# Attention with a feed-forward layer on one Trainium2 core: two scalars spread by a matmul, another opening order, and eight weight slices prepared in fewer steps

## The chip, the cores and the metric

The kernel runs on one core of a Trainium2 chip. The time is the device time of one execution in microseconds (us), given as the median of several. The core's engines have queues of their own: TensorE multiplies matrices (PE in the profile, with PEld for its weight loads), VectorE (DVE) and ScalarE (ACT) work element by element, GpSimd (POOL) does so too, and SyncE (SP) issues most DMAs. Each engine takes its instructions in the order in which the program lists them.

## The reference

Local attention with a few global keys, and then a feed-forward layer without a gate. Cut to what matters:

```python
B, H, S, D = 4, 8, 768, 64                     # n_global = 8, n_local = 96
scores = q @ k.T / sqrt(D) - slopes * dist     # per head; dist from the diagonal, n_local for global keys
keep = (pos_k < n_global) | ((rel >= 0) & (rel < n_local))
a = softmax(where(keep, scores, -1e9))
x = (a @ v) as (B * S, H * D)                  # 3072 x 512
h = x @ w_in                                   # 512 x 2048
out = where(h > 0, h, exp(min(h, 0)) - 1) @ w_out
```

All data is float64 or float32 on the host; w_in and w_out arrive as float64 and are turned into float32 on the chip. n_global and n_local are two int64 values that the kernel reads at run time.

## The kernel before, in words

The 3072 rows are 12 groups of 256. A group's attention is done in 4 pairs of heads: a load of q and k (tile qk) and of v (tiles v, u), a scaling of q (L449 to L453), 16 score matmuls (s, L474), a fused add-and-minimum against a table of distances (pr, L462, DVE), an exponential with a running sum (L464, ACT), a reciprocal, a normalisation (L449 to L453), transposes on PE (t), their copies (pt) and the product with v (pv). The result is kept as two float32r parts (xh, xl), since a float32 product is made of three float32r ones.

The feed-forward layer's weights are 16 slices each of w_in and w_out, 512 KB of float64 bits a slice (tile bits). `weight` turns a slice into float32 in seven steps: ACT takes the absolute value of the high words read as float32 (L393), DVE or POOL clamps it (L395), DVE shifts it left by 3 and masks it (L396), DVE puts the sign and top bit back (L398) and the upper bits of the low words in (L400), then the high part is copied (w HI, L303 or L305) and the low part subtracted (w LO, L311, POOL).

A planner (`Plan`) sets the order on every engine: each operation has a due time, costs on the engines that may run it, and tiles with a list of slots; the planner simulates and writes down the order that it finds. It starts from numbers for when each engine (FREE) and the DMA stream (BW0) become free. SP's queue is one list: a DMA that waits holds back all that are listed after it. The first three groups are computed while the weights are prepared (the opening); from then on groups alternate between the two matmul layers, and the last eight groups use `seven`, a product with seven instead of eight terms, whose mixed weights (mix) are loaded again for each group.

Ahead of the planned work stands `setup`. It builds the two distance tables far0 and far1 and a small table tabg, which need n_global and n_local. The two scalars come by a DMA that spreads 16 bytes over 128 partitions (n_raw, issued on ACT's queue, L232), are turned to float32 (n_up, n_val, L240 and L242) and applied to the tables (L364 to L372). PE meanwhile runs eight matmuls on a tile of ones (none<-fill, L1113), which compute nothing that is used. Later, where the planner foresees PE idle for more than a bound, further such fills are put in (L1106 and L1113).

At the end a flag is summed from checks of the data; if one fails, a slow path (`dense`) recomputes everything. With this input it is not taken.

Of the kernel before, what the change touches and what calls it, by code (L numbers as in the profile page):

```python
# [8 lines left out]
F32 = mybir.dt.float32  # L9
# [50 lines left out]
class Plan:  # L60
# [5 lines left out]

    BW0 = 2250.0

    FREE = {"PE": 5200.0, "ACT": 3600.0, "DVE": 5300.0, "POOL": 6000.0, "SP": 700.0}

# [165 lines left out]
def scalars(nc, pool, raw):  # L236

    n = raw.shape[1]
    up = pool.tile([P, n], F32, name="n_up")
    nc.vector.scalar_tensor_tensor(up, raw[:, :, 0], 0.0, raw[:, :, 1], ALU.is_lt, ALU.add)  # L240
    val = pool.tile([P, n], F32, name="n_val")
    nc.vector.scalar_tensor_tensor(val, up, float(2 ** 32), raw[:, :, 0], ALU.mult, ALU.add)  # L242
    return [val[:, i:i + 1] for i in range(n)]


class Kernel:
# [67 lines left out]
    def consts(self):  # L314
        self.ident = self.const("ident", [P, P])
        self.far0, self.far1 = self.const("far0", [P, LW]), self.const("far1", [P, LW])

        self.scale = self.const("scale", [P, self.NP])
        if self.ON_PE:
            self.minus1 = self.const("minus1", [P, P], F32R)  # L320
        self.nmax = self.const("nmax", [P, self.B * self.H * self.S // P])
        self.zero = self.const("zero", [P, W], F32R)
        self.sums = {x: self.c.tile([P, 2 * NT, 4], F32, name=x) for x in self.SLOTS["st"]}

    def setup(self):
# [15 lines left out]
        nc.scalar.activation(t, t, AF.Exp)  # L341
        if self.WARM:
            self.fill = m.tile([P, 512], F32R, tag="xh2a", name="fill")
            nc.vector.memset(self.fill.bitcast(F32), 1.0)
            self.none = self.ps.tile([P, 512], F32, tag="h1", name="none")

        for r, at in halves:
# [6 lines left out]
        nc.scalar.copy(far0, far1)  # L354
        nc.vector.tensor_copy(g, j)
        for h in range(0, self.H, 2):
            nc.gpsimd.memset(self.scale.t[:, h // 2:h // 2 + 1], self.q_scale(h))
        nc.gpsimd.tensor_scalar(self.scale.t[HW:], self.scale.t[HW:], 2.0, 1.0, ALU.mult, ALU.mult)
        for r, at in halves:
            nc.gpsimd.memset(far0[r, :at - 32], -BIG)  # L360
            nc.gpsimd.memset(far0[r, at:at + NG], -BIG)
        self.ng, self.nl = scalars(nc, self.c, self.raw)
        ng, nl = self.ng, self.nl
        nc.vector.tensor_scalar(d, d, nl, -BIG, ALU.is_ge, ALU.mult)  # L364
        nc.vector.tensor_scalar(g, g, ng, -BIG, ALU.is_ge, ALU.mult)
        nc.vector.tensor_tensor(far0, far0, d, ALU.add)
        nc.vector.tensor_scalar(g, g, nl, None, ALU.subtract)
        nc.vector.tensor_tensor(far1, far1, d, ALU.add)
        for r, at in halves:
            x = far0[r, at - 32:at - 32 + NG]  # L370
            nc.vector.tensor_tensor(x, x, g[r], ALU.max)
            nc.gpsimd.tensor_copy(far1[r, at:at + NG], g[r])  # L372
        make_identity(nc, self.ident.t)
        nc.gpsimd.memset(self.zero.t.bitcast(F32), 0.0)
        if self.ON_PE:
            nc.scalar.activation(self.minus1.t, self.ident.t, AF.Copy, scale=-1.0)
        for x in self.sums.values():
            nc.gpsimd.memset(x[:, :, 1], 1e-9)


    def weight(self, which, fc, due, after):
# [10 lines left out]

        p.add((("ACT", 575.0, False),), lambda e: nc.scalar.activation(gf(), high().bitcast(F32), AF.Abs), [bits], [g], due - 6000)  # L393
        p.add(dve(DM, True) + (("POOL", 640.0, True),),
              lambda e: self.on(e).tensor_scalar(gf(), gf(), F64_MAX, F64_MIN, ALU.min, ALU.max), [g], [g], due - 5500)  # L395
        p.add(dve(DM, True), lambda e: nc.vector.tensor_scalar(g.t, g.t, 3, 0x3FFFFFFF, ALU.logical_shift_left, ALU.bitwise_and),  # L396
              [g], [g], due - 5000)
        p.add(dve(DM, port=True), lambda e: nc.vector.scalar_tensor_tensor(g.t, high(), -0x40000000, g.t, ALU.bitwise_and, ALU.bitwise_or),  # L398
# [22 lines left out]


    def pair(self, b, gi, hp, xh, xl, due, step, X):
        nc, p = self.nc, self.plan
# [4 lines left out]
        loads = [p.add(sp(), lambda e: nc.sync.dma_start(qk.t, src[:, :W + KS]), writes=[qk], due=due - 9000, nbytes=P * (W + KS) * 4)]  # L429
        loads += [p.add(sp(), lambda e: nc.sync.dma_start(v.t, src[:, W + KS:W + KS + VC]), writes=[v], due=due - 9000, nbytes=P * VC * 4)]  # L430
        if hp % 2 == 0:
            u = self.rest = self.sb("u", "u", [P, VC], slots=X.get("u"))
            loads += [p.add(sp(), lambda e: nc.sync.dma_start(u.t, src[:, W + KS + VC:]), writes=[u], due=due - 9000, nbytes=P * VC * 4)]
        u = self.rest
# [494 lines left out]
    def build(self):  # L929
# [47 lines left out]
        for (n, f0, f1), d in zip(segs, dues):  # L977
            def moe(n=n, f0=f0, f1=f1, d=d):
                b, gi = groups[n]
                if f0 == 0 and f1 < NFC:  # L980
                    parts[n] = [self.sb("part", "part", [P, self.DM]) for _ in range(NT)]
                if n >= self.SE:
                    self.seven(b * self.S + gi * W, *X[n], d, self.STEP, n == len(groups) - 1)
                    return
                self.moe(b * self.S + gi * W, *X[n], f0, f1, d, self.STEP, parts.get(n), n < self.NE, n == len(groups) - 1)
            todo.append((d[f0], moe))
        self.kept, self.mixed = {}, {}
        for j in range(NFC // 2):
# [4 lines left out]
        for _, f in sorted(todo, key=lambda x: x[0]):  # L993
# [28 lines left out]
    SLOTS = {"qk": ["rqv0", "qk0"], "v": ["va1", "va2"], "u": ["rk0", "va0"], "s": ["s0", "s1"], "t": ["t0"], "pv": ["v0", "t0"], "h": ["h0", "h1"], "o0": ["o0"], "o1": ["o1"],  # L1022
             "pr": ["pr0", "pr1", "pr2", "pr3"], "tr": ["pt0", "pt1"], "pt4": ["ph0", "ph1"], "dd": [f"dd{i}" for i in range(4)], "st": [f"st{i}" for i in range(6)], "pt": ["pt0", "pt1"],
             "x": ["x0"], **{x + c: [f"{x}{n}{c}" for n in range(3)] for x in ("xh", "xl") for c in "ab"}, "e": ["e0", "e1"], "gh": ["gh0", "gh1", "gh2"],
             "gl": ["gl0", "gl1", "gl2"], "io": ["io0", "io1", "io2", "io3"], "part": [f"pa{i}" for i in range(6)], "mix": [f"pa{i}" for i in range(6)],  "hl": ["xh0a", "xh0b"], "tf": ["tf0", "tf1", "xl0a", "xl0b"],
             "g": ["io2", "io3"], "sum7": ["ph2", "x0"], "rh": ["gh0", "gh1"], "rl": ["gl0", "gl1"], "sh": ["xh2a", "xl2a"], "sl": ["xh2b", "xl2b"], "o2": ["v0"], "o3": ["t0"], "o4": ["s0"], "o5": ["s1"]}
# [11 lines left out]
    def run(self):  # L1038
# [3 lines left out]
        with self.tc.manual_schedule():  # L1042
# [4 lines left out]
            self.setup()  # L1047
            free = self.warm(self.COLD * 240.0, 0.0)
            cold = min(op.n for op in order if op.eng == "PE" and op.allocs and op.allocs[0].cls == "h")
# [68 lines left out]
    def flag(self):  # L1118
# [10 lines left out]
        nc.vector.tensor_scalar(f[:, 5:6], f[:, 5:6], 1.0, None, ALU.is_lt)  # L1129
        nc.vector.tensor_reduce(f[:, 6:7], f[:, 0:6], axis=AX.X, op=ALU.max)  # L1130
        one = c.tile([P, 1], F32, name="one")
# [3 lines left out]
    def flag_sum(self, flags):  # L1135
        nc, c = self.nc, self.c
        f, one = flags
        s = self.ps.tile([P, 1], F32, tag="s0", name="flagsum")
        nc.tensor.matmul(s[0:1, :], f[:, 6:7], one, start=True, stop=True)
# [113 lines left out]
    def restored(self):  # L1253
        M = self.DM // 2
        for j, x in self.kept.items():
            self.nc.sync.dma_start(self.ws[1][2 * j].t[:, :, M:].bitcast(F32), x.t)

    def dense(self, b):
        for t0 in range(0, self.S // P, NT):
            self.dx = [self.p.tile([P, self.NCC, W], F32R, tag=f"dx{i}", name=self.n("dx")) for i in range(2)]  # L1260
            for i in range(NT):
                self.dense_tile(b, t0 + i, i)
            self.dense_moe(b, t0)

# [77 lines left out]
```

## Time and profile before

| | us |
|---|---|
| median of 3 runs (lowest to highest) | 645.14 (643.47 to 645.53) |
| the profiled execution, time | 644.23 |
| the profiled execution, span | 642.4 |
| PE busy | 631.0 (98%) |
| DVE busy | 492.7 (77%) |
| ACT busy | 411.0 (64%) |
| POOL busy | 199.1 (31%) |

The span is the stretch from the profile's first instruction to its last; the execution's time is 1.8 us more. PE's busy time counts the fills too, and a matmul counts as busy until its modelled end.

### The profile page before, as it was taken

The numbers are of one execution on the slowest core, as the hardware profiler recorded it, in microseconds if no ns is written. First come the engines' busy times: TensorE is split into PE (matmuls) and PEld (weight loads), VectorE is DVE, ScalarE is ACT, GpSimd is POOL, SyncE is SP. The second block draws the span as 40 slices with busy tenths as digits, with TensorE's granted clock in tenths as the row PEclk, the third lists the DMA queues.
The fourth block names the chain that finished last, engine by engine and source line by source line (L and its number), as shares of the span: only waits on it lengthen the run. The fifth ranks groups of instructions, "written<-read, shape, count | busy, mean of one in ns | idle before, by whom it ended". The sixth has DMA issues, their size and how long they took to land.

```text
span 642.4 us, 19164 instructions
## 1 busy us (share of the span) xinstructions
PE 631.0 (98%) x7054; PEld 584.4 (91%) x7054; DVE 492.7 (77%) x1648; ACT 411.0 (64%) x1201; POOL 199.1 (31%) x500
## 2 busy tenths in 40 slices
PE   8999999999999999999999999999999999999996
PEld 5878888898888889999999999999999999999996
DVE  6999888899878975777777777777686777776654
ACT  6999776666644665666666566576566566654553
POOL 3557465465467672121121121112022022020000
PEclk9999999999999999999999999999999999999998
DMA  8979934231365899788888888888888788875542
GB/s 309 376 283 408 342 84 125 70 108 62 87 220 211 260 300 295 250 269 246 270 252 282 258 251 264 277 259 253 273 253 243 254 283 260 277 233 165 181 149 86
DMA packets 131171, 149.82 MB, mean 233 GB/s; under 512 B 63616, under 2 KB 82816, under 8 KB 131072
## 3 DMA queue, kind: packets, MB, share of 16 engines
q1 hardware_dynamic: 130784, 148.41, 71.7%
q8 instruction: 57, 0.93, 0.6%
q14 instruction: 42, 0.34, 0.2%
q10 hardware_dynamic: 288, 0.13, 0.1%
HBM read 117.57 MB, written 30.93 MB: 231 GB/s over the span
## 4 chain that ended last, share of the span: by engine, by line
PE 89%; DVE 4%; ACT 3%; DMA 2%; issue 1%; POOL 0%; DVEq 0%; POOLq 0%; ACTq 0%
PE h L712 28%; PE o L768 24%; PE o L880 13%; PE h L854 12%; PE s L610 5%; PE s L474 4%; PE pv L507 2%; DMA qk<-in_qkv_dram 1%; ACT pr L464 1%; PE t L527 1%; DMA n_raw<-in_n_dram 1%; DVE pr L462 1%; DMA mixed<-mix 1%; PE t L529 0%; DVE g L395 0%
## 5 line engine op out<-in xcount | busy, mean ns | idle before, releaser
L712 PE MATMUL h<-xh,w 128*128 128x256 f32 x1024 | 142.2, 280 | 0.8 <-DVE gg L722 0.8
L712 PEld LDWEIGHTS h<-xh,w 128*128 128x128 f32 x1024 | 129.8, 188 | 3.0 <-issue 1.2
L722 DVE SCALAR_TENSOR_TENSOR gg<-e,h 128x256 f32<-128x256 f32 x128 | 53.4, 417 | 76.0 <-ACT e L721 74.9
L580 POOL TENSOR_SCALAR pr<-pr,st 128x168 f32<-128x168 f32 x144 | 62.6, 435 | 152.1 <-DVE st L482 139.3
L464 ACT ACTIVATE pr<-pr,nmax 128x168 f32<-128x168 f32 x192 | 81.8, 427 | 16.9 <-DVE nmax L462 16.3
L720 ACT ACTIVATE e<-h 128x256 f32<-128x256 f32 x128 | 48.7, 381 | 58.4 <-PE h L712 58.4
L854 PEld LDWEIGHTS h<-xh,w 128*128 128x128 f32 x512 | 76.9, 188 | 9.9 <-DVE h L862 0.2
L880 PE MATMUL o<-w,gh 128*128 128x512 f32 x256 | 81.6, 400 | 0.4 <-DVE ob L912 0.4
L712 PE MATMUL h<-xl,w 128*128 128x256 f32 x512 | 81.8, 281 | 0.0
L854 PE MATMUL h<-xh,w 128*128 128x256 f32 x512 | 81.5, 282 | 0.0
L712 PEld LDWEIGHTS h<-xl,w 128*128 128x128 f32 x512 | 69.4, 188 | 2.0 <-issue 1.7
L462 DVE CUSTOM_DVE_ANT_0 pr<-s,far 128x168 f32<-128x168 f32 x192 | 53.3, 325 | 11.8 <-ACT xh L303 11.1
L311 POOL TENSOR_TENSOR w<-g,w 128x256 fp32r<-128x256 f32 x64 | 50.8, 816 | 35.7 <-ACT w L303 29.8
L303 ACT CAST sh<-sum 128x512 fp32r<-128x512 f32 x64 | 39.8, 621 | 30.9 <-DVE sum L736 30.9
L585 DVE STREAM_TRANSPOSE tr<-pr 128x192 f32<-128x192 f32 x144 | 50.0, 364 | 11.2 <-POOL pr L580 10.7
L721 ACT ACTIVATE e<-e 128x256 f32<-128x256 f32 x128 | 53.4, 417 | 3.6
L768 PE MATMUL o<-mix,sh 128*128 128x256 f32 x256 | 51.1, 281 | 0.0
L880 PEld LDWEIGHTS o<-w,gh 128*128 128x128 f32 x256 | 43.0, 188 | 7.9 <-ACT e L860 1.0
L451 POOL TENSOR_SCALAR qk<-qk,scale 128x256 f32<-128x256 f32 x14 | 8.0, 570 | 135.6 <-DMA qk<-in_qkv_dram 68.1
L311 DVE TENSOR_TENSOR sl<-sum,sh 128x512 fp32r<-128x512 f32 x64 | 44.2, 691 | 5.7 <-ACT sh L303 5.7
L768 PE MATMUL o<-w,sh 128*128 128x256 f32 x256 | 48.1, 280 | 0.0
L303 ACT CAST rh<-gg 128x384 fp32r<-128x384 f32 x64 | 32.8, 513 | 20.1 <-DVE gg L722 19.5
(142 smaller groups left out, 1418.9 us busy)
## 6 DMA issues: line engine op xcount, KB each, us to landing
mix<-mixed SPq DMA_DIRECT2D x192, 256.0 KB, 4.6
qk<-in_qkv_dram SPq DMA_DIRECT2D x48, 312.0 KB, 4.1
v<-in_qkv_dram SPq DMA_DIRECT2D x36, 384.0 KB, 5.0
dd<-tr SPq DMA_DIRECT2D x36, 384.0 KB, 4.6
pt<-dd SPq DMA_DIRECT2D x72, 192.0 KB, 3.8
bits<-in_w_in_dram SPq DMA_DIRECT2D x16, 512.0 KB, 8.5
bits<-in_w_out_dram SPq DMA_DIRECT2D x16, 512.0 KB, 9.7
mixed<-mix SPq DMA_DIRECT2D x32, 256.0 KB, 3.2
```

The source lines that it names most:

```text
L303: self.nc.scalar.copy(out, x)
L311: self.on(e).tensor_tensor(out, x, y, ALU.subtract)
L462: first = p.add((("DVE", 85 + 1.042 * LW, False),), lambda e: nc.vector.tensor_tensor_reduce(x(), s.t[:, i, :LW], tab, -(2.0 ** -(h + 1)), ...
L464: p.add(act(LW, extra=200), lambda e: nc.scalar.activation(x(), x(), AF.Exp, bias=nm, scale=-1.0, accum_out=st.t[:, n, 0:1]), [pr], [pr, s ...
L580: nc.gpsimd.tensor_scalar(pr.t[:, :LW], pr.t[:, :LW], st.t[:, n, 3:4], 1.0, ALU.mult, ALU.mult)
L585: nc.vector.transpose(tr.t[:, :, i, j], pr.t.rearrange("p (b r) -> p b r", r=32))
L712: nc.tensor.matmul(h.t, w1.t[:, s, cc * P:(cc + 1) * P], self.chunk(x, cc), start=n == 0 and s == HI and cc == 0, stop=n == 1 and cc == se ...
L721: p.add(act(W), lambda e: nc.scalar.activation(ex.t, ex.t, AF.Exp, scale=-1.0), [ex], [ex], d - 8000)
L722: p.add(dve(W), lambda e: nc.vector.scalar_tensor_tensor(gs(), ex.t, -1.0, h.t, ALU.add, ALU.max), [h, ex], [g], d - 8000)
L768: nc.tensor.matmul(acc[bank].t[:, half], a, b.t[:, LO if t == 1 else HI, x], start=j == 0 and t == 0 and n in first, stop=j == self.NFC // ...
L854: nc.tensor.matmul(h.t, w1.t[:, s, cc * P:(cc + 1) * P], self.chunk(x, cc), start=n == 0 and cc == 0, stop=n == 2 and cc == self.NCC - 1)
L880: nc.tensor.matmul(o.t[:, :at.stop - at.start], g.t[:, i * P:(i + 1) * P], w2.t[:, s, at], start=fc == f0 and n == 0 and s == HI, stop=fc ...
```

## The change

**Scalars.** n_raw is loaded into one partition. n_up and a new n_one are made there; a matmul with the tile of ones (fill) spreads the two values over 128 partitions (n_all in PSUM), and DVE copies them out (n_val). The eight fills at the start become three ahead of this matmul and two behind it.

**Opening order.** Work on tabg moves from DVE to POOL; the identity and the zero tile are made ahead of the scalars' arrival; far1 is finished behind far0. The planner's FREE and BW0 are smaller, and the first group's v and u loads have due times 9000 later, so that a second qk load stands ahead of them.

**Weights.** For the slices 0 to 3 of w_in and of w_out (BARE = 4, eight slices) the absolute value (L393) and the clamp (L395) are left out, and the shift (L396) reads the high words straight out of the raw bits.

**Check.** From planner time 251000 on, every 12000, half a slice of those raw words is loaded again (tile seen, 16 loads of 256 KB), and ACT runs two activations over its 256 high words a partition with a running sum into a column of `wide`. `flag` takes 32 columns into its result with 4 more DVE instructions. The slow path gets a function `rewritten` that prepares the eight slices in full; it is not run here.

```diff
-    BW0 = 2250.0
-    FREE = {"PE": 5200.0, "ACT": 3600.0, "DVE": 5300.0, "POOL": 6000.0, "SP": 700.0}
+    BW0 = 1200.0
+    FREE = {"PE": 4100.0, "ACT": 3000.0, "DVE": 4400.0, "POOL": 4600.0, "SP": 700.0}
...
-    raw = pool.tile([P, n, 2], I32, name="n_raw")
-    nc.scalar.dma_start(raw, src.bitcast(I32).rearrange("(o n w) -> o n w", o=1, w=2).broadcast_to([P, n, 2]))
+    raw = pool.tile([1, n, 2], I32, name="n_raw")
+    nc.scalar.dma_start(raw, src.bitcast(I32).rearrange("(o n w) -> o n w", o=1, w=2))
...
+    one = pool.tile([1, n], F32, name="n_one")
+    nc.vector.scalar_tensor_tensor(one, up, float(2 ** 32), raw[:, :, 0], ALU.mult, ALU.add)
+    all_ = psum.tile([P, n], F32, tag="h0", name="n_all")
+    nc.tensor.matmul(all_, ones[0:1, :P], one, start=True, stop=True)
     val = pool.tile([P, n], F32, name="n_val")
-    nc.vector.scalar_tensor_tensor(val, up, float(2 ** 32), raw[:, :, 0], ALU.mult, ALU.add)
+    nc.vector.tensor_copy(val, all_)
...
+        self.warm(self.COLD[0] * 240.0, 0.0)
+        self.ng, self.nl = scalars(nc, self.c, self.raw, self.fill.bitcast(F32), self.ps)
+        ng, nl = self.ng, self.nl
+        nc.gpsimd.tensor_scalar(g, g, ng, -BIG, ALU.is_ge, ALU.mult)
+        nc.gpsimd.tensor_scalar(g, g, nl, 0.0, ALU.subtract, ALU.add)
+        nc.vector.tensor_scalar(d, d, nl, -BIG, ALU.is_ge, ALU.mult)
+        nc.vector.tensor_tensor(far0, far0, d, ALU.add)
...
+        bare = fc < self.BARE
+        if not bare:
+            p.add((("ACT", 575.0, False),), lambda e: nc.scalar.activation(gf(), high().bitcast(F32), AF.Abs), [bits], [g], due - 6000)
+            p.add(dve(DM, True) + (("POOL", 640.0, True),),
+                  lambda e: self.on(e).tensor_scalar(gf(), gf(), F64_MAX, F64_MIN, ALU.min, ALU.max), [g], [g], due - 5500)
+        p.add(dve(DM, True), lambda e: nc.vector.tensor_scalar(
+            g.t, high() if bare else g.t, 3, 0x3FFFFFFF, ALU.logical_shift_left, ALU.bitwise_and), [bits if bare else g], [g], due - 5000)
...
+    def watch(self, k, due):
...
+        src = (self.w_in, self.w_out)[which][fc].bitcast(I32)[:, half * DM:(half + 1) * DM]
+        x = self.sb("seen", "seen", [P, DM], I32)
+        p.add(sp(), lambda e: nc.sync.dma_start(x.t, src), writes=[x], due=due - 4000, nbytes=P * DM * 4, early=due - 4000)
...
+        p.add(act(DM // 2, extra=200), lambda e: nc.scalar.activation(t(), t(), AF.Abs, accum_out=w[:, k:k + 1]), [x], [x], due, slack=8000.0)
+        p.add(act(DM // 2, extra=200), lambda e: nc.scalar.activation(t(), t(), AF.Exp, scale=-512.0, accum_out=w[:, n + k:n + k + 1]), [x], [x], due)
...
-    GATE, COLD = 900.0, 8
+    GATE, COLD = 900.0, (3, 2)
...
+    BARE, WATCH = 4, (255000.0, 12000.0)
```

On DVE's queue the opening stood thus before, from the third table step (far is a distance table, tabg the small table) to the first fused step of attention (L462):

```order
L353 SCALAR_TENSOR_TENSOR far_71<-d,after 128x168
L355 CAST tabg<-tabj 128x8
L240 SCALAR_TENSOR_TENSOR n_up<-n_raw 128x2
L242 SCALAR_TENSOR_TENSOR n_val<-n_up,n_raw 128x2
L364 TENSOR_SCALAR d<-d,n_val 128x168
L365 TENSOR_SCALAR tabg<-tabg,n_val 128x8
L366 TENSOR_TENSOR far_70<-far_70,d 128x168
L367 TENSOR_SCALAR tabg<-tabg,n_val 128x8
L368 TENSOR_TENSOR far_71<-far_71,d 128x168
L371 TENSOR_TENSOR far_70<-far_70,tabg 64x8 x2
L462 ISA pr_184,nmax<-s_168,far_70 128x168
```

and thus in the changed program, on the same queue:

```order
L356 SCALAR_TENSOR_TENSOR far_71<-d,after 128x168
L240 SCALAR_TENSOR_TENSOR n_up<-n_raw 1x2
L242 SCALAR_TENSOR_TENSOR n_one<-n_up,n_raw 1x2
L246 COPY n_val<-n_all 128x2
L374 TENSOR_SCALAR d<-d,n_val 128x168
L375 TENSOR_TENSOR far_70<-far_70,d 128x168
L378 TENSOR_TENSOR far_70<-far_70,tabg 64x8 x2
L379 TENSOR_TENSOR far_71<-far_71,d 128x168
L473 TENSOR_SCALAR qk_151<-qk_151,scale 128x256
L482 ISA pr_183,nmax<-s_166,far_70 128x168
```

The three steps on tabg have left DVE; a copy that waits for PE has come in, and so has the scaling of the second pair's q (L473), which before stood on POOL (L451) behind the memsets.

On ACT's queue of the changed program the first of the sixteen checks stands thus in the late stage (e is the activation of the feed-forward layer, rh and sh its rounded parts, seen the raw words):

```order
L307 CAST rh_4599<-gg_4517 128x384
L307 CAST sh_4605<-sum_915_4585 128x512
L469 ACTIVATE qk_4529<-qk_4529,scale 128x256
L740 ACTIVATE e_4629<-h_4590 128x256
L440 ACTIVATE seen_4390,wide<-seen_4390 128x256
L741 ACTIVATE e_4629<-e_4629 128x256
L441 ACTIVATE seen_4390,wide<-seen_4390 128x256
L740 ACTIVATE e_4658<-h_4615 128x256
L741 ACTIVATE e_4658<-e_4658 128x256
```

The two rows of seen are new; they stand between the two steps of e, and between one e and the next.

## Rows read from the trace of the kernel before

**Rows 1.** The page: an engine's busy time over the whole span.

```profile
PE 631.0 (98%) x7054; PEld 584.4 (91%) x7054; DVE 492.7 (77%) x1648; ACT 411.0 (64%) x1201; POOL 199.1 (31%) x500
```

**Rows 2.** Waits of PE after the opening: releaser, us in total, times, longest.

```profile
PE h L712 <- DVE gg L722: 0.8, 1, 0.8
PE o L880 <- DVE ob L912: 0.4, 1, 0.4
```

**Rows 3.** Busy time in three stretches; then clock, DMA share, GB/s.

```profile
core 0: us, PE busy (x) PEld busy (x) DVE busy (x) ACT busy (x) POOL busy (x), PEclk, DMA share, GB/s
6.00:46.00 40.00, 37.88 (x503) 29.19 (x504) 36.68 (x159) 36.24 (x127) 20.31 (x44) 1.00 0.92 344
46.00:60.00 14.00, 13.90 (x198) 11.28 (x198) 13.24 (x51) 13.38 (x49) 11.36 (x17) 1.00 1.03 410
250.00:450.00 200.00, 200.00 (x2493) 193.51 (x2492) 147.04 (x541) 128.27 (x374) 32.04 (x132) 1.00 0.84 261
```

**Rows 4.** The same view for the fills alone (tile none): PE, PEld.

```profile
6.00:46.00 40.00, 6.87 (x28) 4.11 (x28) 1.00 0.92 344
```

**Rows 5.** Timeline of the first 9 us: start, duration, engine, what, idle before.

```profile
0.83 0.40 ACTq L232 DMA_DIRECT2D n_raw<-in_n_dram  x1
...
1.55 3.78 PE L1113 MATMUL none<-fill 128*128 128x512 f32 x8 [1.55 <-DVE fill L344]
...
2.46 0.33 DVE L353 SCALAR_TENSOR_TENSOR far<-d,after 128x168 f32<-128x168 f32 x1
...
4.92 0.16 DVE L240 SCALAR_TENSOR_TENSOR n_up<-n_raw 128x2 f32<-128x2 int32 x1 [2.05 <-DMA n_raw<-in_n_dram]
...
5.32 0.31 DVE L364 TENSOR_SCALAR d<-d,n_val 128x168 f32<-128x168 f32 x1
5.32 0.51 ACT L449 ACTIVATE qk<-qk,scale 128x256 f32<-128x256 f32 x1 [2.16 <-DMA qk<-in_qkv_dram]
...
5.88 1.21 PE L474 MATMUL s<-qk 64*64 64x168 f32 x16 [0.56 <-ACT qk L449]
...
6.89 0.33 DVE L462 CUSTOM_DVE_ANT_0 pr<-s,far 128x168 f32<-128x168 f32 x1
...
8.02 0.48 POOL L451 TENSOR_SCALAR qk<-qk,scale 128x256 f32<-128x256 f32 x1
...
8.56 0.80 PE L474 MATMUL s<-qk 64*64 64x168 f32 x16 [0.34 <-POOL qk L451]
```

**Rows 6.** DMA queues in the first 5 us: packets, MB, share.

```profile
q1 hardware_dynamic: 224, 0.48, 33.6%
q10 hardware_dynamic: 144, 0.00, 1.3%
```

**Rows 7.** DMA issues of the page: count, KB, us from issue to landing.

```profile
mixed<-mix SPq DMA_DIRECT2D x32, 256.0 KB, 3.2
```

**Rows 8.** Groups by line, 10 to 46 us: busy us, mean ns | idle before.

```profile
L393 ACT ACTIVATE g<-bits 128x512 f32<-128x512 f32 x8 | 5.2, 671 | 0.0
L398 DVE SCALAR_TENSOR_TENSOR g<-bits,g 128x512 int32<-128x512 int32 x6 | 4.2, 706 | 0.1
...
L395 POOL TENSOR_SCALAR g<-g 128x512 f32<-128x512 f32 x5 | 3.0, 614 | 1.8 <-ACT g L393 1.7
L396 DVE TENSOR_SCALAR g<-g 128x512 int32<-128x512 int32 x6 | 2.4, 416 | 0.0
L395 DVE TENSOR_SCALAR g<-g 128x512 f32<-128x512 f32 x3 | 2.0, 680 | 0.0
```

**Rows 9.** Groups by line on ACT, 255 to 440 us.

```profile
L721 ACT ACTIVATE e<-e 128x256 f32<-128x256 f32 x60 | 25.0, 417 | 1.6
...
L464 ACT ACTIVATION_READ_ACCUMULATOR pr<-pr,nmax 128x1 f32 x64 | 12.0, 188 | 0.0
```

**Rows 10.** Timeline of the late stage: sl is made, and read next.

```profile
273.69 0.69 DVE L311 TENSOR_TENSOR sl<-sum,sh 128x512 fp32r<-128x512 f32 x1
...
276.66 0.19 PEld L768 LDWEIGHTS o<-mix,sl 128*128 128x128 f32 x1
```

More of the change, by code (lines that the diff above doesn't have):

```diff
@@ L341, in setup @@
         nc.scalar.activation(t, t, AF.Exp)
[L342 to L345, printed above, removed]
+        self.fill = m.tile([P, 512], F32R, tag="xh2a", name="fill")
+        nc.vector.memset(self.fill.bitcast(F32), 1.0)
+        self.none = self.ps.tile([P, 512], F32, tag="h1", name="none")
         for r, at in halves:
@@ L361, in setup @@
             nc.gpsimd.memset(far0[r, at:at + NG], -BIG)
[L362 to L372, printed above, removed]
         make_identity(nc, self.ident.t)
@@ L376, in setup @@
             nc.scalar.activation(self.minus1.t, self.ident.t, AF.Copy, scale=-1.0)
+        self.warm(self.COLD[0] * 240.0, 0.0)
[5 more added lines that the diff above has]
+        nc.vector.tensor_tensor(far0, far0, d, ALU.add)
+        for r, at in halves:
+            x = far0[r, at - 32:at - 32 + NG]
+            nc.vector.tensor_tensor(x, x, g[r], ALU.max)
+        nc.vector.tensor_tensor(far1, far1, d, ALU.add)
         for x in self.sums.values():
             nc.gpsimd.memset(x[:, :, 1], 1e-9)
+        for r, at in halves:
+            nc.gpsimd.tensor_copy(far1[r, at:at + NG], g[r])
     def weight(self, which, fc, due, after):
@@ L429, in pair @@
         loads = [p.add(sp(), lambda e: nc.sync.dma_start(qk.t, src[:, :W + KS]), writes=[qk], due=due - 9000, nbytes=P * (W + KS) * 4)]
-        loads += [p.add(sp(), lambda e: nc.sync.dma_start(v.t, src[:, W + KS:W + KS + VC]), writes=[v], due=due - 9000, nbytes=P * VC * 4)]
+        loads += [p.add(sp(), lambda e: nc.sync.dma_start(v.t, src[:, W + KS:W + KS + VC]), writes=[v], due=due - 9000 + X.get("later", 0), nbytes=P * VC * 4)]
         if hp % 2 == 0:
             u = self.rest = self.sb("u", "u", [P, VC], slots=X.get("u"))
-            loads += [p.add(sp(), lambda e: nc.sync.dma_start(u.t, src[:, W + KS + VC:]), writes=[u], due=due - 9000, nbytes=P * VC * 4)]
+            loads += [p.add(sp(), lambda e: nc.sync.dma_start(u.t, src[:, W + KS + VC:]), writes=[u], due=due - 9000 + X.get("later", 0), nbytes=P * VC * 4)]
         u = self.rest
@@ L986, in build @@
             todo.append((d[f0], moe))
+        for k in range(4 * self.BARE):
+            d = self.WATCH[0] + k * self.WATCH[1]
+            todo.append((d - 4000.0, lambda k=k, d=d: self.watch(k, d)))
         self.kept, self.mixed = {}, {}
@@ L1047, in run @@
             self.setup()
-            free = self.warm(self.COLD * 240.0, 0.0)
+            free = self.warm(self.COLD[1] * 240.0, 0.0)
             cold = min(op.n for op in order if op.eng == "PE" and op.allocs and op.allocs[0].cls == "h")
@@ L1138, in flag_sum @@
         s = self.ps.tile([P, 1], F32, tag="s0", name="flagsum")
-        nc.tensor.matmul(s[0:1, :], f[:, 6:7], one, start=True, stop=True)
+        nc.tensor.matmul(s[0:1, :], f[:, 7:8], one, start=True, stop=True)
         fi = c.tile([1, 1], I32, name="flagint")
@@ L1256, in restored, with rewritten @@
             self.nc.sync.dma_start(self.ws[1][2 * j].t[:, :, M:].bitcast(F32), x.t)
+    def rewritten(self):
+        nc, p, DM = self.nc, self.p, self.DM
+        for fc in range(self.BARE):
+            for which in range(2):
+                bits = p.tile([P, 2 * DM], I32, tag="bits", name=self.n("bits"))
+                g = p.tile([P, DM], I32, tag="bg", name=self.n("bg"))
+                w = self.ws[which][fc].t
+                gf = g.bitcast(F32)
+                words = bits.rearrange("p (n w) -> p n w", w=2)
+                nc.sync.dma_start(bits, (self.w_in, self.w_out)[which][fc].bitcast(I32))
+                nc.scalar.activation(gf, words[:, :, 1].bitcast(F32), AF.Abs)
+                nc.vector.tensor_scalar(gf, gf, F64_MAX, F64_MIN, ALU.min, ALU.max)
+                nc.vector.tensor_scalar(g, g, 3, 0x3FFFFFFF, ALU.logical_shift_left, ALU.bitwise_and)
+                nc.vector.scalar_tensor_tensor(g, words[:, :, 1], -0x40000000, g, ALU.bitwise_and, ALU.bitwise_or)
+                nc.vector.scalar_tensor_tensor(g, words[:, :, 0], 29, g, ALU.logical_shift_right, ALU.bitwise_or)
+                nc.scalar.copy(w[:, HI], gf)
+                nc.vector.tensor_tensor(w[:, LO], gf, w[:, HI], ALU.subtract)
     def dense(self, b):
@@ L1275, in tile_kernel @@
                 f.restored()
+                f.rewritten()
                 with tc.For_i(0, f.B, 1) as b:
```

27 lines of the change are left out of this document (16 added, 11 removed).

## The prediction

> **What bounds the kernel now.** I read the page first: PE is busy for 631.0 us of a span of 642.4 [rows 1]. That alone doesn't say that PE is the limit, since its fills count as work, so the list of PE's waits comes next. After 70 us PE waits for named releasers for 1.2 us in all, in two waits [rows 2]. From there on a change can hardly win anything on DVE, ACT or POOL, and it can lose only if it makes PE wait.
>
> The opening is another matter. The table by stretches for 6 to 46 us shows PE "busy" for 37.88 of 40 us [rows 3], but the same view for the fills alone has 6.87 us of it [rows 4]. So 40 - 37.88 + 6.87 = 9.0 us of PE's time in this stretch do no work that is used. In the same 40 us DVE is busy for 36.68 (92%) and ACT for 36.24 (91%), POOL for 20.31 [rows 3]: two engines that hand each other softmax steps and weight steps are nearly full. From 46 to 60 us PE is at 13.90 of 14 [rows 3] without fills. PE's later work is a fixed queue, so what is won in the opening, by starting sooner or by giving DVE and ACT less to do, moves everything behind it by as much, up to the 9.0 us plus what the start gives.
>
> The start itself is read in the timeline. DVE has its tables prepared at 2.46 + 0.33 = 2.79 and then waits until 4.92 for n_raw; ACT waits 2.16 us for the first qk load, until 5.32; the first fused step of attention on DVE is at 6.89, and the second pair's scores are only at 8.56, behind a scaling that POOL does at 8.02 [rows 5].
>
> **Part 1, the scalars and the opening order.** n_raw was issued at 0.83 and released DVE at 4.92, 4.1 us later [rows 5]. In the first 5 us the queue that carries it moved 144 packets with almost no bytes, against 224 packets of the data queue [rows 6]: spreading 16 bytes over 128 partitions costs 144 of the first 368 packets. With one partition nearly all of these go away. How soon n_raw then lands no row shows. It cannot help before 2.79, when DVE comes free; a transfer of 256 KB takes 3.2 us from issue to landing [rows 7], so 0.83 + 3.2 = 4.0 is a late bound. I take the middle, 3.4.
>
> The DMA: Bandwidth & Descriptors page of the Trainium skill (Anatomy of one DMA) puts the fixed part of a DMA at about 2.0 us, as measured for those that GpSimd issues. By it n_raw would land at about 2.8, at the early bound, and this part would be worth 0.6 us more.
>
> From there: n_up and n_one take 0.40, as n_up and n_val did between 4.92 and 5.32 [rows 5]. Then the new trip through PE, which no row shows: at least 0.3 us (two handovers and a tiny matmul), at most the 1.21 us of the first sixteen score matmuls [rows 5]; a two-column matmul is nearer the low end, 0.5. The fills ahead of it are three of eight that took 3.78 [rows 5], about 1.4 us from 1.55, and are over by then. The copy n_val is about 0.17. From the step on d to the fused step it took 6.89 - 5.32 = 1.57 before [rows 5]; two steps on tabg that leave DVE take about 0.3 of that, and the scaling of the second pair's q, now on DVE ahead of the fused step, adds about 0.35. The sum is 3.4 + 0.40 + 0.5 + 0.17 + 1.27 + 0.35 = 6.1, so 0.8 us sooner, with ends at 5.3 and 7.4 (1.6 us sooner to 0.5 later). The first qk must be there too. It was at 5.32, and with over a third of the packets gone it comes no later; it doesn't decide. What gains more is the second pair: its scaling is done at about 5.8 in place of 8.50, if its load, now second in SP's queue and not fourth, has landed, and its scores follow the first sixteen at about 6.5 to 7, not at 8.56. Between the 0.8 of the first step and the 1.5 to 2 of the second I take **-1.5 us** for the start, bounds -2.1 and +0.5.
>
> **Part 2, the eight weight slices.** All eight are prepared between 10 and 46 us, since the absolute value stands there eight times [rows 8]. What goes: on ACT 8 x 0.671 = 5.4 us; the clamp three times on DVE, 3 x 0.680 = 2.0, and five times on POOL, 5 x 0.614 = 3.1 [rows 8]. What comes: the shift now reads every second word. It took 0.416 on packed words; the step that reads the same high words (L398) takes 0.706 [rows 8]. Between 0 and 0.29 more for each of eight, I take the row that reads the same data: +2.3 us on DVE. So ACT and DVE together lose 5.4 + 2.0 - 2.3 = 5.1 us of work, and POOL 3.1. The planner may give normalisations, scalings and copies to either ACT or DVE, so the relief can be shared: 5.1 / 2 = 2.6 for two engines, (5.1 + 3.1) / 3 = 2.7 if POOL takes its part. The bounds are 0 (DVE alone decides, as it gets +2.3 - 2.0) and 5.4 (ACT alone decides). I take **-2.7 us**; with the start it is well below the 9.0 us that PE can give.
>
> **Part 3, the check in the late stage.** 16 loads of 256 KB and 32 activations. One activation over 256 elements is 0.417 us and its sum's read 0.188 [rows 9], 0.6 together, so 32 x 0.6 = 19 us on ACT within some 190 us, where ACT is busy for 128 of 200 [rows 3]. The loads add 4.2 MB where 261 GB/s x 200 us = 52 MB are moved at a share of 0.84 [rows 3], which becomes about 0.91. What hides them is PE's distance to its inputs. Where four softmax steps already stand among the steps of e, sl is finished at 273.69 + 0.69 = 274.38 and read at 276.66 [rows 10], 2.3 us to spare; a check puts in at most 1.2 us. Queued behind a check that waits for its load is the next e, and for that PE waits; the load is listed on SP about two rounds of mix loads ahead of the round in which it is read. I take **+0.2 us**. Without that cover it would be 16 x 1.2 = 19 us, the upper bound.
>
> The 4 more DVE instructions of the flag stand where DVE is busy for 147 of 200 us [rows 3] and PE doesn't wait: nothing, or under 1 us if that slack were gone. The slow path isn't run.
>
> **The sum.** -1.5 - 2.7 + 0.2 = -4.0 us. The profiled execution took 644.23, so its like would take 640.2. The median of the runs is 0.9 above that execution, 645.14; from it I get **641.1**, and I give 641.0. A difference below 0.3%, 1.9 us, can't be told from none here, so faster means below 643.2.
>
> **The rivals.**
>
> *The loads set the pace.* From 46 to 60 us the DMA share is 1.03, over 6 to 46 it is 0.92 at 344 GB/s [rows 3]. If q, k, v and bits come no sooner, ACT and DVE wait for data with the time they gained, and only what the start moves is kept: -1.3, 643.8, no difference. Against it: the bytes of the opening are the same, and their stream starts with fewer packets. It decides if POOL's and DVE's waits for qk or bits grow by over 2 us.
>
> *The check makes PE wait* (the case on the other side). Two activations are put between two steps of e. If each check held PE up by 0.6 us, one activation, that is 16 x 0.6 = 9.6; with -4.2 for the rest it is +5.4, 650.5. It decides from 4.2 / 16 = 0.26 us a check on. Against it: the 2.3 us to spare, and only 1.2 us of waits after the opening [rows 2, 10].
>
> *PE's clock stays low for longer.* The eight fills end 3.78 us after they began, about 0.43 us apart, which is 512 columns at 1.2 GHz, and the first sixteen score matmuls take 1.21 us against 0.80 for the second [rows 5]: the clock rises to its other level, 2.4 GHz, about then. The changed start has five fills with a wait among them. If the rise came later, each of about five groups of PE work up to 11 us would cost 0.4 us more, 2 us in all: 643.1. The page TensorE: Matmul & The Clock Gate of the Trainium skill (Part 1: The HAM clock gate) says that the array's clock is halved unless it has been busy of late, so that fewer fills speak against the change; the first rows agree that a start from rest is slow.
>
> *More comes of it.* If ACT alone decided, part 2 would be worth 5.4 and the start 2.1: -7.3, 637.8.
>
> **How the numbers follow.** Forecast 0.64, loads 0.14, check 0.08, clock 0.06, more 0.08. The likeliest case alone reaches from 638.8 to 643.0 (2 us for the split of the relief and the start). For 8 in 10 I add the case of the loads and half of the larger gain: 638.0 to 644.5. Faster: the forecast, "more" and half of the clock's and a little of the loads' case, 0.77; the same 0.15; slower 0.08.
>
> **What would show it.** Start: n_raw's wait on DVE ends before 4.0, the first fused step stands at about 6, the second pair's scores before 7.5. Relief: L393 and L395 gone from 10 to 46 us but for later slices, the shift of the eight at 0.6 to 0.7 us, fills plus idle PE from 6 to 46 us at 5 to 6 us in place of 9.0. Check: PE's waits after 70 us still near 1 us. It would be wrong if fills and idle time stay at 9 us (the loads), or if PE waits for gg or sl after each check.

## The result and the profile after

The changed kernel takes 648.4 us (median of 9 executions, 644.81 to 650.4) against 645.14 us before (9 executions on the same chip). The ratio is 1.0056 (95% interval 1.0036 to 1.0076): 3.6 us slower by the ratio, 3.3 by the medians. The forecast was 641.0 (638.0 to 644.5). The profiled execution is the fastest of the nine, 644.81 with a span of 642.9, so its rows show less of the loss than the median has.

The page's busy line (compare [rows 1]) and PE's waits from 70 to 640 us (compare [rows 2]; columns as there):

```profile
PE 629.1 (98%) x7034; PEld 582.5 (91%) x7034; DVE 489.7 (76%) x1639; ACT 417.5 (65%) x1258; POOL 198.5 (31%) x505
```

```profile
PE s L630 <- DMA pt<-dd: 1.5, 3, 0.7
PE o L900 <- ACT e L880: 1.2, 2, 0.7
PE s L630 <- DVE tr L605: 0.3, 1, 0.3
```

PE's waits rise from 1.2 to 3.0 us, and none stands behind gg or sl, where the rival of the check was looked for. They stand at products with v, whose input pt comes back from DRAM (tr is stored as dd and loaded again as pt), and at e in the stage of the mixing.

The table by stretches (columns of [rows 3]), and then the fills alone (compare [rows 4]):

```profile
6.00:46.00 40.00, 37.86 (x501) 28.52 (x498) 36.61 (x156) 35.09 (x129) 19.86 (x38) 1.00 0.95 352
46.00:60.00 14.00, 13.55 (x189) 11.49 (x188) 12.65 (x46) 12.57 (x44) 10.47 (x16) 1.00 1.03 408
186.00:250.00 64.00, 61.86 (x606) 54.11 (x605) 50.36 (x147) 36.48 (x115) 41.58 (x76) 1.00 0.75 239
250.00:450.00 200.00, 198.96 (x2475) 192.19 (x2475) 145.36 (x536) 136.25 (x429) 33.05 (x136) 1.00 0.90 286
```

```profile
6.00:46.00 40.00, 4.68 (x13) 2.10 (x13) 1.00 0.95 352
```

From 6 to 46 us, 40 - 37.86 + 4.68 = 6.8 us of PE do nothing used, where 9.0 did. But from 250 to 450 us PE is idle for 1.04 us, where it had no gap. The stretch from 186 to 250 us, which the prediction did not look at, has 61.86; the same row of the kernel before is

```profile
186.00:250.00 64.00, 63.63 (x621) 56.02 (x620) 51.71 (x150) 35.35 (x112) 41.29 (x80) 1.00 0.82 265
```

so PE is idle there for 1.8 us more. A last part lies behind PE: from the start of its last matmul to the end of the span 6.80 us pass, where 6.05 passed before. The traces have 6.0 to 6.3 us there in the kernel before, e2, e6, e7 and e12, and 6.8 to 7.2 in the others; what sets it stays open. The timeline of the start (compare [rows 5]):

```profile
0.84 0.53 ACTq L232 DMA_DIRECT2D n_raw<-in_n_dram  x1
...
2.73 0.14 DVE L240 SCALAR_TENSOR_TENSOR n_up<-n_raw 1x2 f32<-1x2 int32 x1
...
3.12 0.58 PE L244 MATMUL n_all<-n_one,fill 1*128 1x2 f32 x2
...
3.75 0.16 DVE L246 COPY n_val<-n_all 128x2 f32<-128x2 f32 x1 [0.69 <-PE n_all L244]
3.84 0.51 ACT L469 ACTIVATE qk<-qk,scale 128x256 f32<-128x256 f32 x1 [0.66 <-DMA qk<-in_qkv_dram]
3.94 0.43 DVE L374 TENSOR_SCALAR d<-d,n_val 128x168 f32<-128x168 f32 x1
...
5.52 0.33 DVE L378 TENSOR_TENSOR far<-far,tabg 64x8 f32<-64x8 f32 x2 [0.67 <-POOL tabg L373]
...
6.40 0.33 DVE L482 CUSTOM_DVE_ANT_0 pr<-s,far 128x168 f32<-128x168 f32 x1
...
6.84 1.21 PE L494 MATMUL s<-qk 64*64 64x168 f32 x16
```

DVE no longer waits for n_raw, the first fused step is 0.49 us sooner, the second pair's scores 1.72 us sooner. In the first 5 us n_raw's queue carries 2 packets (144 in [rows 6]), and the first qk releases ACT at 3.84, 1.5 us sooner. The shift of the bare slices, in the groups by line from 10 to 46 us, costs what it did on packed words (0.416 in [rows 8]):

```profile
q10 hardware_dynamic: 2, 0.00, 0.0%
```

```profile
L403 DVE TENSOR_SCALAR g<-bits 128x512 int32<-128x512 int32 x7 | 2.8, 418 | 0.1
```

**Where the lead goes.** PE's work is compared by number: the start of the n-th h<-xh,w matmul (1536 in each trace) minus its start in the trace of before, in us, negative when ahead. The columns say when that matmul starts in the trace of before. Each row is one execution: the changed kernel's and e3's are the fastest of their runs, e1's and e9's near the slowest. Runs e1 to e16 follow below.

| profiled execution | 73 | 181 | 242 | 279 | 318 | 471 | 631 |
|---|---|---|---|---|---|---|---|
| changed | -3.3 | -3.3 | -0.7 | -0.8 | -0.8 | 0.2 | -0.2 |
| changed again (e5) | -2.9 | -2.9 | -0.5 | 0.0 | 1.1 | 3.6 | 3.7 |
| no check (e1) | -3.8 | -3.7 | -1.7 | 0.7 | 1.1 | 2.5 | 2.3 |
| mixing earlier (e3) | -3.0 | -3.0 | -3.2 | -3.2 | -1.4 | -2.0 | -1.8 |
| no check, mixing earlier (e11) | -3.2 | -3.2 | -3.6 | -3.6 | -3.4 | -3.4 | -3.9 |
| mixing earlier, small check (e13) | -1.9 | -1.9 | -2.1 | -2.1 | -1.2 | -2.6 | -3.1 |
| mixing earlier, full loads, small activations (e14) | -1.8 | -1.8 | -2.1 | -2.1 | -0.3 | -0.7 | -0.6 |
| weights only (e4) | 1.8 | 1.7 | 1.8 | 1.8 | 3.6 | 2.2 | 1.5 |
| opening only (e6) | 1.4 | 1.7 | 1.4 | 1.3 | 2.0 | 1.2 | 0.7 |
| PE held (e7) | -2.9 | 0.8 | 2.7 | 3.3 | 3.7 | 6.2 | 6.1 |
| small check (e9) | -2.1 | -2.1 | 0.8 | 1.8 | 2.7 | 2.8 | 2.5 |
| full loads, small activations (e10) | -2.0 | -2.0 | 1.6 | 2.9 | 3.4 | 4.1 | 3.8 |

The opening gives 3.3 us (2.9 in e5, the same kernel again) and PE holds them to 181 us. The changed kernel loses them in two places: the mixing (186 to 245 us) and the stage after it (280 to 440 us).

### The profile page after: what moved, and what is told of

It is laid out like the page before. It is cut to its first block, busy times and chain, and to the rows that moved or that the text cites. A ratio compares the mean times of both kernels' runs of the same rounds, so it can differ in the third digit from the quotient of the medians.

```text
span 642.9 us, 19209 instructions
## 1 busy us (share of the span) xinstructions
PE 629.1 (98%) x7034; PEld 582.5 (91%) x7034; DVE 489.7 (76%) x1639; ACT 417.5 (65%) x1258; POOL 198.5 (31%) x505
## 4 chain that ended last, share of the span: by engine, by line
PE 84%; DMA 4%; DVE 4%; POOL 3%; ACT 2%; issue 2%; SPq 0%; POOLq 0%; DVEq 0%; ACTq 0%
PE h L732 27%; PE o L788 24%; PE o L900 11%; PE h L874 10%; PE s L630 4%; PE s L494 4%; PE pv L527 2%; DMA dd<-tr 2%; DMA pt<-dd 1%; POOL pr L600 1%; DVE mix L315 1%; PE t L547 1%; ACT pr L484 1%; PE none L1137 1%; DMA qk<-in_qkv_dram 1%
## 5 line engine op out<-in xcount | busy, mean ns | idle before, releaser
L315 POOL TENSOR_TENSOR w<-g,w 128x256 fp32r<-128x256 f32 x64 | 48.8, 786 | 42.1 <-ACT w L307 29.0
L471 POOL TENSOR_SCALAR qk<-qk,scale 128x256 f32<-128x256 f32 x14 | 6.7, 478 | 150.4 <-DMA qk<-in_qkv_dram 75.8
```

Source lines behind the costliest of these rows:

```text
L315: self.on(e).tensor_tensor(out, x, y, ALU.subtract)
```

## The experiments

Each run's ratio is to the kernel before on the same chip (medians there 644.11 for e1 to e4, 644.42 for e5 to e8, 645.59 for e9 to e12, 644.31 for e13 to e16). The ratios weigh all executions and are up to 0.0013 off the quotient of the two medians. e13 has 5 executions, e5, e7 and e12 have 6, e10 has 8, the others 11 or 12.

| run | us | ratio (95%) |
|---|---|---|
| e1 no check | 646.51 | 1.0024 (1.0003 to 1.0044) |
| e2 before, with the check | 645.58 | 1.0023 (1.0007 to 1.0040) |
| e3 mixing earlier | 646.34 | 1.0028 (1.0008 to 1.0048) |
| e4 weights only | 644.60 | 1.0006 (0.9989 to 1.0022) |
| e5 changed, again | 648.78 | 1.0080 (1.0052 to 1.0108) |
| e6 opening only | 643.31 | 0.9986 (0.9970 to 1.0003) |
| e7 PE held | 650.58 | 1.0099 (1.0077 to 1.0121) |
| e8 check from 90 us, mixing earlier | 646.61 | 1.0037 (1.0023 to 1.0052) |
| e9 small check | 644.84 | 0.9997 (0.9974 to 1.0020) |
| e10 full loads, small activations | 650.12 | 1.0083 (1.0055 to 1.0111) |
| e11 no check, mixing earlier | 641.94 | 0.9950 (0.9932 to 0.9968) |
| e12 opening only, mixing earlier | 652.01 | 1.0098 (1.0066 to 1.0129) |
| e13 = e3, small check | 640.47 | 0.9941 (0.9927 to 0.9955) |
| e14 = e3, full loads, small activations | 644.42 | 1.0004 (0.9989 to 1.0018) |
| e15 check by 165 us, mixing earlier | 644.67 | 1.0014 (0.9996 to 1.0032) |
| e16 check by 165 us | 643.89 | 0.9990 (0.9970 to 1.0010) |

**The parts alone.** e1 takes the loop over `watch` out of the changed kernel and sets `wide` to zero (the check of those words is left out). e2 is the kernel before with `watch` and the longer flag. e4 is the kernel before with `bare` in `weight` (no check of those words). e6 is the changed kernel with

```diff
-        bare = fc < self.BARE
+        bare = False
```

and no check, which full preparation does not need.

> The changed kernel without the sixteen late loads of raw words and their 32 activations (the columns of the flag that they fill are set to zero instead, so nothing is checked). Theory C (the check costs: its 4.2 MB and 19 us of ACT work make PE wait in the last eight groups): the time falls by 3 to 4 us against the changed kernel, to 644 to 645.5, and the runs lie as close together as those of the kernel before. Theory M (the lead of 3.3 us that the changed kernel has from 70 to 186 us is lost between 186 and 245 us, where the mixed weights are made at fixed planned times and their stores stand in SP's queue between the transfers dd and pt): the lead is still lost by 245 us, and the time stays within 1 us of 648.4.

> The kernel before with the check alone added (sixteen loads, 32 activations, the longer flag; scalars, opening and weights as before). C: 3 to 4 us slower than the kernel before, 648 to 649, with a wider spread. M: within 1 us of the kernel before, 645.

> The kernel before with the eight slices prepared without absolute value and clamp, and nothing else of the change (no check). A lead of about 2 us at 100 us (the change's 3.3 less the start's 1.1). C: the lead reaches the end, 643. M: it is lost between 186 and 245 us, 645.

> The changed kernel with all weight slices prepared as before and without the check (its columns are set to zero): only the scalars, the opening order and the planner's new starting numbers are left. A lead of 1 to 2 us at 100 us. M: lost by 245 us, as the planned times of the mixing stand still; time within 1.5 us of the kernel before. If leads were kept, 1 to 2 us below the kernel before.

The check costs 1.5 us on the kernel before (0.0023 x 644; 0.5 to 2.6 by the interval). Taking it out of the changed kernel leaves 1.0024, between what the two theories expected: the check is not all of the loss. Neither part of the opening wins much alone: against the leads that were expected, PE is behind the kernel before at 73 us in both e4 and e6. In these two executions the opening's matmuls came late to their full rate (sixteen score matmuls take 1.40 us at 9.13 in e4, eight take 0.84 at 9.57 in e6, where sixteen take 0.80 at 8.56 before), and in e4 the granted clock fell again (last section), so the two runs do not price the parts.

**The place of the mixing.** e3 changes one number in the changed kernel:

```diff
-    PREPARE, SE = (168000.0, 9000.0, 6000.0), 4
+    PREPARE, SE = (164000.0, 9000.0, 6000.0), 4
```

It sets the due times of the step that mixes the weights for `seven` (hl, tf, mix, mixed). e7 asks whether the loss there comes from absolute times: PE runs 31 more matmuls on zeros, at 106 us and for 3.7 us in the trace, and gives up its lead ahead of the mixing.

> The changed kernel, with the mixing of the weights planned 4 us earlier (164000 in place of 168000), by about the lead. M: the lead of 3.3 us is kept to within 1 us at 245 us, and the time is 2 to 3 us below the changed kernel's, 645.5 to 646.5. C: the lead at 245 us may change but the end stays near 648.

> The changed kernel itself once more, for a second profile and more executions beside the others. All theories: 2 to 4 us slower than the kernel before; a lead near 3.3 us from 70 to 186 us that is gone by 245 us (theory M: lost where the weights are mixed), and after that waits of PE for loads of mix and pt in other places than in the first profile (theory D: late transfers).

> The changed kernel, with 31 matmuls of zeros added on PE once, at about 97 us, which hold PE back by 3.3 us, about the lead (nothing that is used is changed). D and M (what follows is paced by transfers and by the mixing, not by PE): the same time as the changed kernel to within 1 us, since the waits between 186 and 245 us shrink by what was added. If PE were the limit to the end: 3.3 us slower than the changed kernel.

In e3 the lead passes 186 to 279 us whole, and in e5 2.9 us of it are gone by then. In e7 PE, now 0.8 us behind at 181, loses another 2.5 by 279. So it isn't that PE runs into work that cannot come sooner: the theory of an absolute pace falls, and the order in which the queues hold the mixing's steps is what costs. (The medians of e7 and e5 are only 1.8 us apart; of the 3.7 us, 3.2 are left at 242 and 2.6 at 471, so the late stage takes up a part.) Two readings show how. The timeline of the changed kernel at 184 us, all engines:

```profile
183.66 1.78 POOL L692 TENSOR_TENSOR hl<-w 128x512 f32<-128x512 f32 x1
...
184.20 1.52 DVE L315 TENSOR_TENSOR mix<-tf,mix 128x256 fp32r<-128x256 f32 x1
...
187.52 0.42 DVE L882 SCALAR_TENSOR_TENSOR h<-e,h 128x256 f32<-128x256 f32 x1
...
188.24 0.39 ACT L880 ACTIVATE e<-h 128x256 f32<-128x256 f32 x1
...
188.68 0.70 PE L900 MATMUL o<-w,gh 128*128 128x512 f32 x2 [0.51 <-ACT e L880]
```

The mixing step on DVE takes 1.52 us, where its like takes 0.41 at 182.86, with POOL idle, and ends 0.28 us behind POOL's step on hl. The page SBUF — State Buffer of the Trainium skill (Who interferes with whom) says that a DVE instruction with two inputs in SBUF contends with a GpSimd instruction that reads SBUF; the trace agrees. Behind it on DVE stand three more mixing steps, and only then the step of h; h, gh and e come late, and PE waits. The long step alone doesn't make the wait. The kernel before has two like it, with h right behind, and PE waits for neither:

```profile
198.40 1.50 DVE L311 TENSOR_TENSOR mix<-tf,mix 128x256 fp32r<-128x256 f32 x1 [0.89 <-POOL mix L305]
199.82 0.42 DVE L862 SCALAR_TENSOR_TENSOR h<-e,h 128x256 f32<-128x256 f32 x1
```

The chain of the changed kernel that ends in PE's wait at 237 us (start, duration, what):

```profile
223.83 0.76 POOL mix L315
...
224.60 0.62 SPq L688
...
225.33 0.55 SPq L716
...
225.97 5.38 DMA dd<-tr
...
232.07 4.94 DMA pt<-dd
...
237.14 0.86 PE s L630 x43
```

SP's queue stood at the store of a mixed slice (L688), which waits for POOL; behind it stood the store of tr to dd, whose way out and back takes over 10 us.

**What of the check costs.** e9 and e10 keep every queue in exactly the changed kernel's order but for a memset of `wide` on POOL, and shrink the work of its entries:

```diff
-    nc.sync.dma_start(x.t, src)
+    nc.sync.dma_start(x.t[0:8], src[0:8])
...
-    nc.scalar.activation(t(), t(), AF.Abs, accum_out=w[:, k:k + 1])
+    nc.scalar.activation(t()[0:8, 0:8], t()[0:8, 0:8], AF.Abs, accum_out=w[0:8, k:k + 1])
```

e9 has both edits (and the like for the second activation), e10 those on the activations only. e13 and e14 are the same pair on e3's order. e11 is e1 and e12 is e6 with the mixing planned earlier.

> The changed kernel with every queue in the changed order, but each of the 16 loads of the check brings 8 partitions instead of 128 and each of the 32 activations covers 8 x 8 elements (the check of those words is left out, so this only prices it). Theory of work: the check's own bytes and activations hold PE up; then the time falls by what the run without a check gave back, 2 us, to about 646.5, and PE's lead over the kernel before at 279 us stays through the late stage. Theory of order: the order of the queues that the planner wrote with the check costs, whatever the check weighs; then 648.3 to 648.8, and the lead is lost between 186 and 330 us as before.

> The same with the 16 loads in full and only the 32 activations shrunk to 8 x 8 elements (the check is left out but for its loads). If the loads' bytes delay the round trips behind PE's waits for pt, this stays near the changed kernel, 648 to 649; if ACT's 19 us are what costs, it comes to the time of the run with both shrunk. Under the theory of order both are within 0.5 us of the changed kernel.

> Mixing planned 4000 earlier, with every queue in the order of that run with its check, but loads of 8 partitions and activations of 8 x 8 elements (the check of those words is left out). If the check's bytes are the cause, this comes to the run without a check, 641.5 to 643; if the order that the check's entries give is the cause, it stays at 646.

> The same order with the 16 loads in full and the activations at 8 x 8 elements. If the bytes are the cause: 646, as with the full check. If ACT's 19 us are: 642 to 643.

> No check at all, and the mixing planned 4000 earlier. If the loss has two separate parts, the mixing (about 2.5 us) and the check (about 2 us), both are gone and PE keeps its 3 us of lead: 641 to 643. If the late waits for transfers come with any plan that differs from the one of before, the lead reaches 279 us and is lost later: 645 to 646.5.

In one order, loads of 16 x 240 KB = 3.9 MB more cost 650.12 - 644.84 = 5.3 us, in the other 644.42 - 640.47 = 4.0. Where the small check stands in for the full one, the order costs nothing in the one (e9 at 0.9997, the run without a check at 1.0024) and nothing in the other (e13 at 0.9941, e11 at 0.9950). So it is the loads. No part of the activations is clear of the noise: e3 less e14 is 0.24%, 1.5 us, with intervals that overlap, and e10 is no faster than the changed kernel. Nor does ACT wait for the loads: in the traces of the changed kernel, e5, e10 and e14 it is never idle for seen. PE's waits from 70 to 640 us, and DMA issues from 186 to 440 us (count, KB each, median us to landing), first of e13:

```profile
PE s L630 <- DMA pt<-dd: 0.6, 1, 0.6
PE o L900 <- DVE ob L932: 0.2, 1, 0.2
```

```profile
mix<-mixed SPq DMA_DIRECT2D x96, 256.0 KB, 4.8
...
dd<-tr SPq DMA_DIRECT2D x19, 384.0 KB, 4.9
```

and then of e14:

```profile
PE s L630 <- DMA pt<-dd: 2.1, 4, 0.8
```

```profile
mix<-mixed SPq DMA_DIRECT2D x95, 256.0 KB, 5.2
...
seen<-in_w_in_dram SPq DMA_DIRECT2D x8, 256.0 KB, 5.3
```

Loads of mix land 0.4 us later with the check's bytes among them, and the waits for pt grow from 0.6 to 2.1 us. That is one pair. Of the profiled executions the e9 and e10 pair shows less, 645.9 and 647.0 of span, than its medians: the waits for pt are 2.6 and 2.5 us, and only e10 waits for mix, 1.1. And bytes are not all that can cost in the late stage: e1, without a check, waits there for mix for 3.3 us and loses 4.2 us of its lead from 242 to 471, as much as e5 with one. So the price of the loads is shown by the medians of two pairs, their way to PE by one pair of traces. With both causes out, e11 and e13 come to 641.94 and 640.47: the forecast time, by a kernel that has no check.

**The check elsewhere.** e8, e15 and e16 keep the whole change and its check, and move the check to where the DMA moves some 100 GB/s (95 from 90 to 165 us in the kernel before); its tiles lie in other buffers, and the planner leaves 4 us, not 8, between load and use. e8 and e15 plan the mixing 4000 earlier, e16 leaves it at its place. e8 uses (90000.0, 6000.0), still running at 186 us.

```diff
-    BARE, WATCH = 4, (255000.0, 12000.0)
+    BARE, WATCH = 4, (92000.0, 4500.0)
...
-"seen": ["rk0", "va0"]
+"seen": ["io2", "io3"]
```

> The changed kernel with the mixing planned 4 us earlier and the check between 86 and 190 us, where the DMA engines have a share of 0.24 to 0.56, instead of 255 to 440 us (its tiles lie in two other buffers, and the planner leaves 4 us, not 8, between load and use). C: what the check costs late, 1.5 to 2 us, is saved, and with the lead kept through the mixing the time falls to 643 to 644.5. D: late transfers still cost 1 to 2 us of the lead, 644.5 to 645.5.

> The whole change with its full check, but the check between 92 and 165 us of the plan, where the DMA moves about 100 GB/s, and the mixing 4000 earlier. If late bytes are the cause, the check is free and this is 641.5 to 643.5. If the opening or the mixing loses time to the new order, PE will wait there for ob or e, and it is 644 to 647.

> The same with the mixing at its planned place. If the late bytes and the mixing's place cost separately, the check costs nothing and the mixing's 2.5 us are lost: 643.5 to 645.5.

> Scalars and opening order alone (full preparation of all slices, no check), with the mixing planned 4000 earlier. Its parent was at 643.3 with a lead of 1.4 us that reached the end nearly whole, so there is little left to win: 642.5 to 643.5 if the mixing's place costs anything there, 643 to 645 if a new order brings waits for transfers of its own.

e16 brings the whole change back to the kernel before (0.9990), 4.3 and 5.8 us below the changed kernel by its two ratios. It was expected to lose 2.5 us at the mixing, and its trace loses 1.3 from 181 to 242. e8 and e12 miss their ranges, and e15 comes out as its second case, all three at one place: with the mixing earlier in these orders, PE waits for ob, 2.8, 4.6 and 1.7 us in all. PE's waits from 186 to 250 us of e12, and DVE's rows ahead of it:

```profile
PE o L901 <- DVE ob L933: 4.6, 3, 3.4
```

```profile
206.86 2.34 DVE L315 TENSOR_TENSOR mix<-tf,mix 128x256 fp32r<-128x256 f32 x2
209.12 0.68 DVE L933 TENSOR_TENSOR ob<-o,part 128x512 f32<-128x512 f32 x1
```

Two mixing steps of 2.34 us together stand ahead of the step that reads PE's accumulator and so frees it. Planning the mixing 4000 earlier is thus no remedy by itself: by the ratios it wins 1.8 us from the changed kernel to e3 (3.4 from e5), 3.6 from e9 to e13, 4.8 from e1 to e11 and 5.1 from e10 to e14, and it loses 1.5 from e16 to e15 and 7 from e6 to e12. What decides is which mixing step the planner puts ahead of which step that PE waits for. A new due time also re-orders what follows, so these differences hold the later stages too.

## Why the prediction was wrong

**The rows of before, and part 1: right in its result, in part by luck.** The first fused step came at 6.40 (forecast 6.1), the second pair's scores at 6.84 (6.5 to 7). n_raw was there when DVE came free at 2.73, at most 1.89 us after its issue; I had taken 3.4. The trip through PE, for which no row of before stood, took 0.70 from n_one's end at 3.05 to the copy at 3.75, where I took 0.5. The steps from d on took 2.46 (3.94 to 6.40), where I took 1.62: DVE waited 0.67 for the work on tabg that the change gives to POOL. The two errors nearly cancel. The DMA: Bandwidth & Descriptors page of the Trainium skill (Anatomy of one DMA), with about 2.0 us, was nearer than the middle of my bounds.

**Part 2: right in kind, and with part 1 about 1 us too large.** The shift cost 0.418 us and not 0.7, so DVE got less work than I had counted. Still fills and idle time fell by 2.2 us, to 6.8 and not to 5 or 6. The clock took a part: the second sixteen score matmuls took 1.21 us, where they took 0.80 [rows 5]. Together parts 1 and 2 were forecast at 4.2 and measured 3.3 as a lead at 73 us. That lead is worth its price where it lasts: e11 and e13 end 0.50% and 0.59% below the kernel before, 3.2 and 3.8 us (e13's trace has 1.9 at 73 us and wins 1.2 more by 631, so its 3.8 is not the opening's alone).

**The step that failed** is the sentence that "PE's later work is a fixed queue, so what is won in the opening, ..., moves everything behind it by as much". The queue is fixed only within one program. The changed program has another order of the mixing's steps against PE's, 140 us behind the end of the opening, and in this order 2.6 us of the 3.3 were gone by 242 us (2.4 in e5; 2.0 to 3.6 in e1, e9 and e10). Neither the weights alone (e4) nor the opening alone (e6) loses anything there; both together do (e1). I read 250 to 450 us, where the check stands, and not 186 to 250, where DVE, POOL and SP carry a one-time job; in the kernel before PE was idle for only 0.37 us there.

**Part 3 was mis-sized**, +0.2 for what measured 1.5 us on the kernel before, 2 to 3.6 in the changed one (e1 against the first and second measurement of it), and 4.0 and 5.3 for the loads alone in the paired orders. I priced the cover of the activations, 2.3 us at sl [rows 10], and let the loads stand as a share that rises from 0.84 to 0.91. As far as one pair of traces shows (e13 and e14), their cost is the delay of other transfers, mix and the way over dd and pt, which has no slack.

**The rivals.** The check as a cause of waits got 0.08, with the time about right (650.5) by another mechanism: not an activation between two steps of e, but bytes among transfers. "PE's clock stays low for longer" came true beside it, by the durations of the matmuls: e9, e10, e13 and e14 have about 1 us less of the lead at 73 us. "The loads set the pace" did not: the DMA share from 6 to 46 us is 0.95, and the lead is there. Open is why the changed kernel's executions differ by 5.6 us among themselves and e9's by 5.9 (those of the kernel before by up to 5.5); the profiled pairs show that waits for pt vary, not what starts it.

## What to carry to other kernels

An order that a planner writes is a part of the kernel: after any edit of its costs or due times, follow PE's lead by the number of its instructions to the end, past every one-time stage, before a gain at the start is counted as a gain at the end. Price a load that is "hidden" by the tightest round trip that shares its queue, not by the mean DMA share. To split an order from the work in it, keep the order and shrink the work.

## What was not expected of the hardware

How soon the opening's matmuls come to their full rate varies, between programs and between executions of one. The score matmuls of e13 on PE:

```profile
4.79 1.40 PE L494 MATMUL s<-qk 64*64 64x168 f32 x16
...
6.89 1.64 PE L494 MATMUL s<-qk 64*64 64x168 f32 x16
...
9.61 0.84 PE L494 MATMUL s<-qk 64*64 64x168 f32 x8
...
13.13 0.52 PE L494 MATMUL s<-qk 64*64 64x168 f32 x8
```

Eight take 0.84 us at 9.61 and 0.52 from 13.13 on, while the changed kernel has 0.52 from 8.64. But the changed kernel run again (e5) has 1.59 us for the sixteen at 6.85, where its first trace has 1.21, so the order of the program isn't the whole cause. The granted clock is given as 1.00 in all these stretches; only the durations show the difference. Later the granted clock itself can fall. The table by stretches of e4, and its timeline:

```profile
30.00:38.00 8.00, 6.67 (x91) 5.15 (x83) 7.79 (x29) 7.52 (x25) 3.71 (x8) 1.00 0.58 173
38.00:46.00 8.00, 7.30 (x69) 6.39 (x70) 5.46 (x20) 5.07 (x18) 3.11 (x7) 0.57 1.00 347
```

```profile
38.70 0.69 PE L529 MATMUL t<-ident,pr 128*128 128x128 f32 x2 [1.76 <-ACT pt L303]
```

The granted clock is 0.57 of full from 38 to 46 us, most of it at the lower of the two levels, 1.2 GHz, after PE had been busy for 6.67 of 8 us and had waited for ACT for the last 1.76 us ahead of 38.70. The two transposes take 0.69 us there and 0.44 at 32.49. A part of a change that only makes PE idle a little more in the opening can pay for it twice.
